# Five slots instead of four for the stacks of split q and k rows, with each load one pair of head pairs further up

## The chip, the cores and the metric

The kernel runs on one core of a Trainium2 chip. The time is device microseconds of one execution, from the first instruction to the last. The engines are called as in the profile: PE is TensorE (matmul) and PEld its weight loads, DVE is VectorE, ACT is ScalarE, POOL is GpSimd, SP is SyncE, which issues nearly all DMAs; SPq is the sequencer of its queue. Each engine runs its instructions in the order in which the program lists them. An instruction that has to wait holds up whatever stands behind it on that engine, and this holds for a DMA that SP issues as well.

## The reference

One transformer block with conditioning. The input is 2048 rows of 512 numbers; attention has 32 heads of 16 and works in four segments of 512 rows, with a memory that is carried from segment to segment.

```python
mod = (_silu(c) @ w_mod).reshape(c.shape[0], 6, 1, -1)          # sa, ca, ga, sb, cb, gb
h = _layernorm(x) * (1 + ca) + sa
x = x + ga * A(h)
h = _layernorm(x) * (1 + cb) + sb
x = x + gb * (gelu(h @ w1 + b1) @ w2 + b2)                      # 512 -> 1792 -> 512

def A(x):                                       # per segment s of 512 rows, per head
    logits = qs @ ks.T * scale + causal_mask
    a_dot  = softmax(logits) @ vs
    a_mem  = (phi(qs) @ M) / (phi(qs) @ z + 1e-6)
    o      = g * a_mem + (1 - g) * a_dot
    M, z   = M + phi(ks).T @ vs, z + sum(phi(ks))
    return concat(o) @ wo
```

## The kernel before

The program has three phases. The first, to about 195 us, does the modulation, the layer norm, the projections to q, k and v and the memory. The rows of q and k are written to DRAM (tiles QD and KD) as three bf16 terms each, so that a bf16 matmul of 96 rows gives a product of the two in higher precision. The third phase, from 495 us, is the feed-forward part.

Between them runs the attention loop. A **stack** is a group of four heads of one segment (two head pairs) whose split q and k rows lie side by side in SBUF; there are 32 stacks, Q = 0 to 31, and 64 head pairs, P = 2Q and 2Q + 1. A stack's rows are loaded by two DMAs (L192) into a slot, which is a pair of tiles `qst` and `kst` of 96 used rows by 4 x 512. Rows 96 to 98 carry the negated row maximum (`m_put`, L676 for q) and ones (for k, filled once per slot by ScalarE, L187). A stack Q uses slot `Q % NK`, with `NK = 4`.

The loop runs over P from -4 to 65. In each step `PRM['order']` lists what every engine gets, in text order: `S` parts compute scores of pair P + 4 (L608, L643) and their row maximum on VectorE (L615), `T` parts compute the transposed scores of pair P (`st_mm`, L694), their exponential on ScalarE (L713, L724) and the causal zeros on GpSimd (L697), and the slots `c0` to `c9` take whatever a table put at position 10P + c. From that table come, among others:

- `load_stacks(Q)` at position 20Q + `PRM['stacks']`, here 20Q - 60, that is at P = 2Q - 6. The first scores of the stack are computed at P = 2Q - 4.
- `pv_part` (L738), the weighted sum of v with a stack's exponentials, and `pv_out`, which evicts it (L131, tile `ts`) and stores it (L749, `TD`).
- for each group U of two stacks: `pv_in` loads sums and denominators back (`dn` L754, `opk` L756) and the memory's part (`amB` L763, and in the last segment its reciprocal denominators `rm` L768); `den` inverts the denominators (L773, L774) and stores them (L776, `RD`); `rb_in` loads them back, spread over 16 rows each (L782, `rbB`); `mem_mix` (L794), `mix` (L787, L789) on GpSimd up to group 12 and on VectorE from 13, `o_hi` (ScalarE, L131, tile `oh`) and `o_lo` (L804) make the output of the group, and `wo_part` (L815) projects it.
- `wo_x` and `wo_out` load x, add the projection and store it (`X2D`, L834).

Memory for the first two slots is taken in the first phase from a ring of four buffers (tag `wm`): qst0, kst0, qst1, kst1. The other slots come at the start of the loop from the pool `wop`. The ring is used again near the end of the loop by `stage_w1` (L839), which stages raw feed-forward weights two blocks at a time; `PRM['w1at']` places `w1r0`, `w1r2`, `w1r4` at P = 58, 59 and 60. They get the ring's buffers in turn: w1r0 that of qst0, w1r2 that of kst0, w1r4 that of qst1. A buffer is handed over when the last instruction that used it has ended; here this is the last L694 of the last stack that used the slot.

Of the kernel before, what the change touches and what calls it, by code (L numbers as in the profile page):

```python
# [41 lines left out]
 'mput': [-14, -15, -13, -13],  # L42
 'mrow0': -19,
 'mput0': -9,
 'stacks': -60,
 'den': [84, 84, 84, 84],
 'dnl': 11,
 'rbl': 7,
# [57 lines left out]
def block_kernel(ctx: ExitStack, tc: tile.TileContext, x, wq, wk, wv, wo, betaq, betam,  # L106
# [22 lines left out]
    def copy(e, dst, src):  # L129
        if e == "a":  # L130
            act.activation(dst, src, AF.Copy)  # L131
        else:
            (v if e == "v" else pool).tensor_copy(dst, src)
# [43 lines left out]
    QD = [[dram.tile([6, 16, 8, 512], BF16, name=f"QD{s}_{g}") for g in range(4)] for s in range(NSEG)]  # L177
    KD = [[dram.tile([6, 16, 8, 512], BF16, name=f"KD{s}_{g}") for g in range(4)] for s in range(NSEG)]
    TERMS = {"q": (slice(0, 3), slice(4, 6), slice(3, 4)), "k": (slice(2, 5), slice(0, 6, 5), slice(1, 2))}
    NK = 4  # L180
    qst, kst = {}, {}

    def new_stack(i, pl=None):
# [5 lines left out]
    def load_stacks(Q):  # L189
        s, g, t = Q // 8, (Q // 2) % 4, Q % 2  # L190
        for st, dd in ((kst[Q % NK], KD), (qst[Q % NK], QD)):
            sp.dma_start(st[:96], dd[s][g].rearrange("c r e n -> (c r) e n")[:, 4 * t:4 * t + 4, :])  # L192
# [393 lines left out]
    with ExitStack() as pb:  # L586
# [69 lines left out]
        def q_of(P, h, i):  # L656
            return qst[P // 2 % NK][:96, 2 * (P % 2) + h, 128 * i:128 * i + 128]

        def k_of(P, h, n):
            return kst[P // 2 % NK][:96, 2 * (P % 2) + h, 0:n]  # L660

# [9 lines left out]
        def m_put(Q):  # L671
# [3 lines left out]
            copy(PRM["mse"], ms, mm[:48, :128])  # L675
            act.dma_start(qst[Q % NK][96:99], ms)  # L676

# [14 lines left out]
        def st_mm(ps, P, h, j):  # L692
            q, k, e = qst[P // 2 % NK], kst[P // 2 % NK], 2 * (P % 2) + h
            pe.matmul(ps, k[:99, e, 128 * j:128 * j + 128], q[:99, e, 128 * j:512], start=True, stop=True)  # L694
# [153 lines left out]
        def at(P, part, f, *a):  # L848
            todo.setdefault((P, part), []).append((f, a))
# [23 lines left out]
        def ap(pos, f, *a):  # L873
            at(pos // 10, pos % 10, f, *a)

        for Q, P in ((2, -4), (3, -2)):
            at(P, 0, new_stack, Q, wop)
        for Q in range(2, 32):
            ap(20 * Q + PRM["stacks"], load_stacks, Q)
# [311 lines left out]
```

## Time and profile before

| what | value |
|---|---|
| time, three runs | 818.09, 818.81, 825.99 us; median 818.81 |
| profiled execution | span 822.1 us; no other time of it is shown |
| PE busy | 795.2 us, 97% |
| DVE, ACT, POOL busy | 498.7, 365.1, 284.7 us |
| DMA moved | 123.02 MB, 150 GB/s on average |
| attention loop, about | 180 to 495 us |
| feed-forward part, about | 495 to 822 us |

A row of a timeline reads: start, length, engine, line, operation, output <- inputs with buffer numbers left out, how many alike in a row, and in brackets the idle time before with the instruction that ended it. A row of the waits reads: who waited, for whom, us in total, times, the longest. On SPq a row is the issue of a DMA and not its transfer.

### The profile page before, as it was taken

How to read it: one execution, taken by the hardware profiler on the slowest of the kernel's cores; microseconds unless marked ns; L12 is line 12 of the kernel's file. 1: busy time of each engine (PE TensorE's matmuls, PEld its weight loads, DVE VectorE, ACT ScalarE, POOL GpSimd, SP SyncE). 2: the span in 40 equal slices, each digit the busy share in tenths (PEclk: the TensorE clock that was granted, in tenths of full speed). 3: DMA queues.
4: the chain of work that ended last, by engine and by line, in shares of the span. 5: the costliest groups of instructions: out<-in, count | busy, mean ns of one | idle time of the engine just before them, and what ended most of it. 6: DMA issues, size and time to landing. Idle time of an engine off the chain costs nothing.

```text
span 822.1 us, 13438 instructions
## 1 busy us (share of the span) xinstructions
PE 795.2 (97%) x4637; PEld 549.7 (67%) x4637; DVE 498.7 (61%) x1341; ACT 365.1 (44%) x670; POOL 284.7 (35%) x508
## 2 busy tenths in 40 slices
PE   9999999999988899989998989999999999999998
PEld 4877777865434345435544547788888888888887
DVE  6685696469877767877787736886443343324223
ACT  4465645565777756766677662223211111211110
POOL 1347365542577545557867651000000000000000
PEclk9999999999999989989999999999999999999999
DMA  9597756595556666667566664734030111003001
GB/s 342 169 312 251 276 183 206 173 360 135 144 144 169 172 182 193 208 187 210 174 172 177 193 185 150 257 103 140 1 103 1 51 51 52 1 0 103 1 1 51
DMA packets 83565, 123.02 MB, mean 150 GB/s; under 512 B 14116, under 2 KB 46244, under 8 KB 82984
## 3 DMA queue, kind: packets, MB, share of 16 engines
q1 hardware_dynamic: 81000, 120.19, 47.2%
q10 hardware_dynamic: 2496, 1.97, 0.8%
q8 instruction: 36, 0.59, 0.3%
q14 instruction: 33, 0.27, 0.1%
HBM read 75.60 MB, written 46.15 MB: 148 GB/s over the span
## 4 chain that ended last, share of the span: by engine, by line
PE 46%; DMA 4%; DVE 2%; ACT 2%; issue 1%; POOL 1%; SPq 1%; ACTq 0%; DVEq 0%
PE acc L1073 17%; PE f1b L989 16%; PE pvb L738 3%; PE att L694 3%; PE att L608 2%; PE mm L815 2%; DMA xb<-in_x 1%; DMA xt<-X2D 1%; ACT pt L713 1%; PE mm L161 1%; DMA rm<-rdd 1%; DMA w1r<-in_w 1%; PE mm L1073 1%; DMA kst<-KD 0%; ACT ts L131 0%
## 5 line engine op out<-in xcount | busy, mean ns | idle before, releaser
L615 DVE CUSTOM_DVE_ANT_0 dump<-att,maskb 128x512 bf16<-128x512 f32 (+2 forms) x384 | 192.2, 552 | 54.9 <-PE att L608 36.5
L713 ACT ACTIVATE pt<-att 128x512 f32<-128x512 f32 x256 | 144.4, 603 | 55.8 <-PE att L694 41.7
L992 ACT ACTIVATE gt<-f1b,b1t 128x512 f32<-128x512 f32 x56 | 38.5, 688 | 245.7 <-PE f1b L989 202.0
L139 DVE CAST gh<-gt 128x512 fp32r<-128x512 f32 x56 | 24.9, 445 | 164.1 <-ACT gt L992 164.1
L697 POOL TENSOR_SCALAR_AFFINE_SELECT pt<-pt 128x256 f32<-128x256 f32 x256 | 98.9, 408 | 54.1 <-ACT pt L713 31.6
L694 PE MATMUL att<-qst,kst 99*128 99x512 bf16 (+3 forms) x512 | 109.2, 306 | 3.3 <-ACT pt L713 2.8
L608 PE MATMUL att<-kst,qst 96*128 96x512 bf16 (+2 forms) x384 | 92.9, 335 | 10.7 <-DMA qst<-QD 8.9
L1073 PE MATMUL acc<-w2h,gh 128*128 128x512 f32 (+1 forms) x224 | 86.6, 387 | 0.0
L1073 PE MATMUL acc<-w2l,gh 128*128 128x512 f32 (+1 forms) x224 | 86.0, 384 | 0.5 <-DVE w2l L140 0.5
L1073 PE MATMUL acc<-w2h,gl 128*128 128x512 f32 (+1 forms) x224 | 85.9, 383 | 0.0
L738 PE MATMUL pvb<-pt,V 128*32 128x512 f32 (+2 forms) x992 | 84.2, 452 | 0.0
L694 PEld LDWEIGHTS <-kst 99*128 99x128 bf16 x512 | 45.2, 99 | 56.4 <-issue 33.1
L989 PE MATMUL f1b<-hodd,w1h 128*128 128x512 f32 x224 | 73.7, 390 | 0.0
L152 POOL TENSOR_SCALAR crs<-cmv 128x4 f32<-128x4 f32 x4 | 1.0, 248 | 172.1 <-DVE cmv L149 172.1
L608 PEld LDWEIGHTS <-qst 96*128 96x128 bf16 x384 | 33.8, 100 | 35.3 <-DMA qst<-QD 11.2
L738 PEld LDWEIGHTS pvb<-pt,V 128*32 128x32 f32 x992 | 25.3, 110 | 45.1 <-issue 41.4
L1073 PEld LDWEIGHTS acc<-w2l,gh 128*128 128x128 f32 x224 | 42.1, 188 | 9.2 <-DVE w2l L140 0.9
L989 PEld LDWEIGHTS f1b<-hodd,w1h 128*128 128x128 f32 x224 | 42.1, 188 | 8.6
L1073 PEld LDWEIGHTS acc<-w2h,gl 128*128 128x128 f32 x224 | 42.1, 188 | 8.3
L1073 PEld LDWEIGHTS acc<-w2h,gh 128*128 128x128 f32 x224 | 42.1, 188 | 8.3
L989 PE MATMUL f1b<-C0hh,w1l 128*128 128x512 f32 x112 | 43.7, 390 | 0.2 <-DVE w1l L140 0.2
L989 PE MATMUL f1b<-C0hl,w1h 128*128 128x512 f32 x112 | 43.7, 390 | 0.0
(214 smaller groups left out, 1540.6 us busy)
## 6 DMA issues: line engine op xcount, KB each, us to landing
kst<-KD SPq DMA_DIRECT2D x32, 384.0 KB
qst<-QD SPq DMA_DIRECT2D x32, 384.0 KB
TD<-ts SPq DMA_DIRECT2D x32, 256.0 KB
QD<-q SPq DMA_DIRECT2D x16, 384.0 KB
KD<-k SPq DMA_DIRECT2D x16, 384.0 KB
wm<-in_wmod SPq DMA_DIRECT2D x20, 256.0 KB
QD<-q SPq DMA_DIRECT2D x16, 256.0 KB
KD<-k SPq DMA_DIRECT2D x16, 256.0 KB
```

What stands on the lines that cost most here:

```text
L139: v.tensor_copy(hi, src)
L161: pe.transpose(ps[:, 128 * b:128 * b + 128], xh[:, b, 128 * d:128 * d + 128], ident)
L608: pe.matmul(ps, q_of(P, h, i), k_of(P, h, 128 * (i + 1)), start=True, stop=True)
L615: v.tensor_tensor_reduce(out=dump[n_dump[0] % 2][:, :n], in0=src, in1=maskb[:, 512 - n:], scale=-1.0, scalar=-4 * NEG, op0=ALU.add, op1=AL ...
L694: pe.matmul(ps, k[:99, e, 128 * j:128 * j + 128], q[:99, e, 128 * j:512], start=True, stop=True)
L697: pool.affine_select(out=t, in_=t, pattern=pattern, compare_op=ALU.is_ge, fill=0.0, base=0, channel_multiplier=-1)
L713: act.activation(pt[:, h, :], ps, AF.Exp, scale=0.25)
L738: pe.matmul(ps[32 * c:32 * c + 32, lo:hi], V[4 * s + j][:, VW * hd:VW * hd + 32], pt[:, c % 2, lo - o:hi - o], start=start, stop=stop)
L815: pe.matmul(ps, a[:, 128 * b:128 * b + 128], w[:, g, :], start=(g == 0 and i == 0), stop=(g == 3 and i == 2))
L989: pe.matmul(ps, a[:, k, :], b[k], start=(i == 0), stop=(i == 11))
L992: act.activation(g, ps, AF.Gelu_apprx_tanh, bias=b1t[:, f:f + 1])
L1073: pe.matmul((mm if lo else acc[b])[:, lo:hi], a[:, c], w[:, lo:hi], start=(f == 0 and i == 0), stop=(last and i == 2))
```

## The change

The load position goes from 20Q - 60 to 20Q - 80 (P = 2Q - 8), there are five slots, and the fifth is made at P = 0 in the pool `wop`.

```diff
- 'stacks': -60,
+ 'stacks': -80,
...
-    NK = 4
+    NK = 5
...
-        for Q, P in ((2, -4), (3, -2)):
+        for Q, P in ((2, -4), (3, -2), (4, 0)):
             at(P, 0, new_stack, Q, wop)
         for Q in range(2, 32):
             ap(20 * Q + PRM["stacks"], load_stacks, Q)
```

What it moves is seen in the order of SP's instructions. In the middle of the loop, at the store of stack 4's sums; KD1_1 and QD1_1 hold stacks 10 and 11, KD1_0 and QD1_0 stacks 8 and 9, and the digit after `kst` or `qst` is the slot. Before:

```order
L192 DMA kst1_1782<-KD1_0_93 96x2048
L192 DMA qst1_1781<-QD1_0_77 96x2048
L749 DMA TD2_2751<-ts4_2752 128x512
L776 DMA RD1_2768<-dn1_2707 128x32
L782 DMA rbB1_2804<-RD1_2768 128x1x512
L192 DMA kst2_2020<-KD1_1_94 96x2048
L192 DMA qst2_2019<-QD1_1_78 96x2048
```

and now, at the same place:

```order
L192 DMA kst0_1777<-KD1_1_94 96x2048
L192 DMA qst0_1776<-QD1_1_78 96x2048
L749 DMA TD2_2756<-ts4_2757 128x512
L776 DMA RD1_2773<-dn1_2712 128x32
L782 DMA rbB1_2809<-RD1_2773 128x1x512
L192 DMA kst1_1782<-KD1_1_94 96x2048
L192 DMA qst1_1781<-QD1_1_78 96x2048
```

The load of stack 10 has moved up to where that of stack 9 stood, past one store of sums (TD) and the pair RD and rbB; stack 11's stands where stack 10's stood. The instructions between keep their order. A load's slot was last used by stack Q - 4 before and by stack Q - 5 now.

At the end of the loop PE's rows keep their order, and only the slots change: pair 61's last transposed scores, a projection, pair 63's first and, after the first v sums of stack 30, its last ones. Before:

```order
L694 MATMUL att4_2010<-qst2_2019,kst2_2020 128x128
L815 MATMUL mm_1983<-woh_1996,oh9_4758 128x512
...
L738 MATMUL pvb_2012<-pt60_0_5561,V12_151 32x512 x2
L738 MATMUL pvb_2012<-pt61_0_5592,V12_151 32x512 x2
...
L694 MATMUL att2_2008<-qst3_2078,kst3_2079 128x128
L738 MATMUL att3_2009<-pt62_0_5647,V12_151 32x512 x2
```

and now:

```order
L694 MATMUL att4_2010<-qst0_1776,kst0_1777 128x128
L815 MATMUL mm_1983<-woh_1996,oh9_4763 128x512
...
L738 MATMUL pvb_2012<-pt60_0_5564,V12_151 32x512 x2
L738 MATMUL pvb_2012<-pt61_0_5595,V12_151 32x512 x2
...
L694 MATMUL att2_2008<-qst1_1781,kst1_1782 128x128
L738 MATMUL att3_2009<-pt62_0_5650,V12_151 32x512 x2
```

Stacks 30 and 31 lay in slots 2 and 3; now they lie in slots 0 and 1, those of the ring. Slot 0's and slot 1's last stacks before were 28 and 29.

The part of SP's order that follows the weights' staging is the same before and after except for the numbers; it reads now:

```order
L839 DMA w1r0_5412<-in_w1 128x4x128 x2
L834 DMA X2D2_123<-xb2_1_5221 128x512
L754 DMA dn13_5449<-TD13_5261 128x1x32
L756 DMA opk13_5451<-TD13_5261 128x1x512
L763 DMA amB13_5453<-AMD3_1_118 128x512
L768 DMA rm13_5455<-rdd3_1968 128x1x512
...
L839 DMA w1r2_5480<-in_w1 128x4x128 x2
L749 DMA TD14_5511<-ts28_5512 128x512
L839 DMA w1r4_5546<-in_w1 128x4x128 x2
L834 DMA X2D2_123<-xb2_2_5341 128x512
L776 DMA RD13_5569<-dn13_5449 128x32
L782 DMA rbB13_5593<-RD13_5569 128x1x512
```

Here w1r0 and w1r4 are the loads whose buffers come from slots 0 and 1; what stands behind them belongs to group 13, to the third segment's output and to stack 28.

## The prediction

> **What bounds the kernel now.** I read the page's busy times first, then the waits of TensorE, then the waits of SyncE's DMA queue, then the timelines of the places that these name. The page, with the span, the busy row and the costliest wait of TensorE's score matmuls:
>
> ```profile
> span 822.1 us, 13438 instructions
> ...
> PE 795.2 (97%) x4637; PEld 549.7 (67%) x4637; DVE 498.7 (61%) x1341; ACT 365.1 (44%) x670; POOL 284.7 (35%) x508
> ...
> L608 PE MATMUL att<-kst,qst 96*128 96x512 bf16 (+2 forms) x384 | 92.9, 335 | 10.7 <-DMA qst<-QD 8.9
> ```
>
> TensorE is busy for 97% of the span, so whatever idle time is taken from it is gained and whatever is added is lost. The program runs it in order, and from 495 us on it is the feed-forward part alone; a delay before that moves the end. The waits of TensorE say what an earlier load can take away at most directly: six waits, 8.9 us.
>
> ```profile
> PE att L608 <- DMA qst<-QD: 8.9, 6, 2.9
> ```
>
> They lie in one stretch. Busy time by stretch (columns: stretch, length, busy time of each engine, granted clock, DMA share, GB/s):
>
> ```profile
> 226.00:304.00 78.00, 68.63 (x545) 31.69 (x543) 54.86 (x206) 52.06 (x105) 46.87 (x99) 0.93 0.61 166
> 304.00:452.00 148.00, 141.75 (x1148) 73.94 (x1146) 114.00 (x420) 101.54 (x202) 99.98 (x195) 0.98 0.65 189
> ```
>
> In 226–304 us TensorE idles 9.4 us and its clock is granted at 0.93; later in the same loop at 0.98. Idle time plus 0.05 × 68.6 = 3.4 us of clock gives 13 us, more than which the head of this loop can't give.
>
> **Part 1: the earlier load, in the head.** The load of stack Q+1 now stands where that of Q stood in SyncE's queue; it waits, as before, for the previous stack of its slot, which with five slots is one stack older. So a load is issued one stack (about two head pairs) sooner, and the six waits for landings (8.9 us) should go. What is late next? SyncE's own queue:
>
> ```profile
> 236.35 0.37 SPq L749 DMA_DIRECT2D TD<-ts  x1
> ...
> 243.55 0.60 SPq L754 DMA_DIRECT2D dn<-TD  x1
> ...
> 247.65 0.34 SPq L776 DMA_DIRECT2D RD<-dn  x1
> 252.82 0.60 SPq L782 DMA_DIRECT2D rbB<-RD  x1
> ...
> 254.48 0.38 SPq L749 DMA_DIRECT2D TD<-ts  x1
> ```
>
> One group of two stacks takes SyncE 254.48 − 236.35 = 18.1 us, and its links are DMA round trips: store TD to load dn 7.2 us, store RD to load rbB 5.2 us. The waits of that queue over the run say the same:
>
> ```profile
> SPq L782 <- DMA RD<-dn: 44.2, 16, 5.0
> ...
> SPq L192 <- PE att L608: 34.1, 15, 14.8
> ```
>
> The slot waits (34.1 us) are what the change shortens; the 44.2 us behind RD stay. And the end of this chain already has a consumer standing there. GpSimd, then ScalarE, in the same group:
>
> ```profile
> 257.31 1.27 POOL L787 TENSOR_TENSOR opk<-opk,rbB 128x512 f32<-128x512 f32 x1 [3.45 <-DMA rbB<-RD]
> ```
>
> ```profile
> 258.62 0.63 ACT L131 ACTIVATE oh<-opk 128x512 fp32r<-128x512 f32 x1 [0.87 <-POOL opk L787]
> ```
>
> GpSimd waited 3.45 us for rbB, and ScalarE 0.87 us for GpSimd, with the exponentials queued behind it. If TensorE came there 2 us earlier per group, ScalarE would wait 2 us longer. I therefore take −4 us, about half of the 8.9 and a third of the 13. The ends are −13 us (all of the loss goes) and 0 (each wait for a load becomes one for rbB).
>
> **Part 2: the fifth slot's fill.** One more fill of 32 rows by ScalarE.
>
> ```profile
> L187 ACT ACTIVATE kst<-one x4: 1887/1904/1905, 161.3 to 188.4; 32x2048 bf16<-32x2048 f32 x4
> ```
>
> It costs 1.9 us on ScalarE at P=0, near 200 us, where the loop's first exponentials are due. ScalarE is busy 44% of the span, so most of it lies beside other work: +0.5 us, between 0 and 1.9. The third extra load in a row in the start (stack 4's) is two DMA issues of about 0.4 us on a queue that then has nothing else due: 0.
>
> **Part 3: the tail.** This is where the sum turns. Slots 0 and 1 share a ring of four buffers with the staging of FFN weights: w1r0 takes the buffer of qst slot 0, w1r2 that of kst 0, w1r4 that of qst 1. Which stack was last in them changes. With four slots, the last in slot 0 is stack 28 and in slot 1 stack 29; with five, they are 30 and 31, the last two of all. So SyncE's w1r0 waited for pair 57's last transposed-score matmul (L694) and now waits for pair 61's; w1r4 waited for pair 59's and now waits for pair 63's, the end of the loop. SyncE is in order. Behind w1r0 stand X2D, dn13, opk13, amB13, rm13, w1r2 and TD14; behind w1r4 another X2D, RD13, rbB13 and all of the last two groups. Before, on SyncE:
>
> ```profile
> 463.25 0.99 SPq L839 DMA_DIRECT2D w1r<-in_w  x2
> 467.51 0.34 SPq L834 DMA_DIRECT2D X2D<-xb  x1
> ...
> 470.49 0.59 SPq L768 DMA_DIRECT2D rm<-rdd  x1
> ...
> 475.31 1.70 SPq L839 DMA_DIRECT2D w1r<-in_w  x2
> ...
> 479.14 0.38 SPq L776 DMA_DIRECT2D RD<-dn  x1
> 483.54 0.60 SPq L782 DMA_DIRECT2D rbB<-RD  x1
> ```
>
> and on TensorE (pair 57's last L694s, pair 61's, the start of stack 30's weighted sum, pair 63's last, stack 31's weighted sum):
>
> ```profile
> 462.25 0.60 PE L694 MATMUL att<-qst,kst 99*128 99x256 bf16 x4
> ...
> 479.62 1.31 PE L694 MATMUL att<-qst,kst 99*128 99x512 bf16 x7
> ...
> 484.21 1.06 PE L738 MATMUL pvb<-pt,V 128*32 128x512 f32 x8
> ...
> 487.40 1.04 PE L694 MATMUL att<-qst,kst 99*128 99x512 bf16 x7
> ...
> 492.03 3.01 PE L738 MATMUL att<-pt,V 128*32 128x512 f32 x28 [2.61 <-POOL pt L697]
> ```
>
> The consumers, on GpSimd, VectorE and ScalarE:
>
> ```profile
> 478.39 1.28 POOL L794 TENSOR_TENSOR amB<-amB,rm 128x512 f32<-128x512 f32 x1 [0.62 <-DMA rm<-rdd]
> ...
> 483.50 1.25 POOL L697 TENSOR_SCALAR_AFFINE_SELECT pt<-pt 128x256 f32<-128x256 f32 x3 [0.57 <-ACT pt L724]
> ```
>
> ```profile
> 487.83 0.69 DVE L787 TENSOR_TENSOR opk<-opk,rbB 128x512 f32<-128x512 f32 x1 [11.43 <-DMA rbB<-RD]
> ```
>
> ```profile
> 489.36 0.63 ACT L131 ACTIVATE oh<-opk 128x512 fp32r<-128x512 f32 x1 [2.49 <-DVE opk L789]
> ```
>
> First hold. w1r0 is released at 479.62 + 1.31 = 480.9 instead of 462.9. It issues for 1.0 us to 482.0; X2D 0.34, dn13 0.6, opk13 0.6, amB13 0.4 bring rm13 to 484.2. From issue to GpSimd's start of L794 it took 478.39 − 470.49 = 7.9 us there, and in the chain of what ended last a later one took 6.1:
>
> ```profile
> 500.16 6.09 DMA rm<-rdd
> ```
>
> So L794 starts at 490.3 to 492.1, lasts 1.28 us, and GpSimd's causal selects of pair 60, three of which stand behind it, take 1.25 us more (as the three at 483.50): stack 30's weighted sum starts at 492.9 to 494.7, middle 493.8, instead of 484.21: +9.6 us. Pair 63's last L694s follow in TensorE's order: 488.44 + 9.6 = 498.0.
>
> Second hold. w1r4 is released at 498.0; it issues in 1.35 us (between the 0.99 and 1.70 above), X2D in 0.34, so that RD13 goes out at about 499.9. Then 483.54 − 479.14 = 4.4 us to rbB13 and 487.83 − 483.54 = 4.3 us to VectorE's mix: 508.6 instead of 487.83, **+20.8 us**. Where these round trips were short, store to load took 2.2 us:
>
> ```profile
> 505.48 0.32 SPq L776 DMA_DIRECT2D RD<-dn  x1
> 507.69 0.59 SPq L782 DMA_DIRECT2D rbB<-RD  x1
> ```
>
> That would make it +18.6. The rest hangs on the mix without slack: ScalarE's oh13 stands ahead of pair 63's exponentials (it waited 2.49 us before too), these gate stack 31's weighted sum, that gates the feed-forward part, which is bound by TensorE to the end.
>
> **Part 4: clock after the two holds.** TensorE idles some 9 to 10 us in each. What a restart costs, from the longest wait in the head:
>
> ```profile
> 278.68 0.50 PE L608 MATMUL att<-kst,qst 96*128 96x384 bf16 x2 [0.73 <-DMA qst<-QD]
> ...
> 281.99 0.39 PE L694 MATMUL att<-qst,kst 99*128 99x512 bf16 x1
> ...
> 289.16 0.82 PE L608 MATMUL att<-kst,qst 96*128 96x384 bf16 x2 [2.95 <-DMA qst<-QD]
> ...
> 293.01 2.36 PE L738 MATMUL pvb<-pt,V 128*32 128x512 f32 x16
> 295.30 0.61 PE L694 MATMUL att<-qst,kst 99*128 99x512 bf16 x1
> ```
>
> The same sequence took 281.99 − 278.68 = 3.3 us after a short wait and 295.30 − 289.16 = 6.1 us after one of 2.95: 2.8 us lost. Against it, the 2.61 us wait at 492.03 shows no such loss. Ends: 0 and 5.7 for two restarts; the holds are long, so they are nearest to the longer wait: +5.7.
>
> The Trainium skill, "TensorE: Matmul & The Clock Gate", section "Part 1: The HAM clock gate", says that TensorE falls to half its clock after about 3.4 us idle and needs about 3.4 us of work to return; an estimate from that is at most 1.7 us lost for each restart, and the sum by it would be 2.3 us lower. This case's trace differs: 2.8 us were lost after only 2.95 us idle.
>
> **Sum.** −4 + 0.5 + 20.8 + 5.7 = +23.0 us on the profiled execution's 822.1 us span. That execution lies inside the three times shown (818.1 to 826.0); on their median, 818.8, it gives **841.8 us**.
>
> **Rivals.**
> A, the forecast: 0.60.
> B, the head gives all it can (−13): speaks for it that SyncE's chain might run ahead once no load holds it; against it, the rbB waits. 818.8 − 13 + 27 = 833: 0.14.
> C, only the first hold counts, because RD13's trip ends beside it: −4 + 0.5 + 9.6 + 2.8 = +8.9, 828: 0.10. Against it stands that w1r4 can't be released before the last L694, which itself comes after the first hold.
> D, everything long: no gain in the head, rm 7.9 us, X2D 1.95 us: +30, 849: 0.06. A part of this is also the case that the change doesn't do what it says, that is that waits for loads only change into waits for rbB: then it is +27, 846.
> E, **faster**: the hold in SyncE's queue doesn't take place, because the weights' load finds its buffer free early. Its point: w1r0 issued before 471 us, where it is past without moving rm13's use at 478.39. Then the head alone counts, −4 to −13, 806 to 815, middle 810. Against it: slot waits do stop SyncE (34.1 us above), and w1r0 went out 0.4 us after pair 57's last L694, as if waiting for it. 0.10.
>
> The Trainium skill, "Perfetto Trace Analysis", section "Identifying Performance Opportunities / Optimization Strategy", reads a gap that repeats on the engine that should be saturated as a possible sign of too few buffers; that speaks for E. The trace agrees in the head (six waits), and is silent on who else uses the buffers.
>
> **How the numbers follow.** A measurement of this kernel can tell about 1% from no change. E below 810.6 is faster, its upper half is the same; C stands on the edge of slower. Faster 0.06, same 0.09, slower 0.85. The range leaves out E and the far end of D, and takes in B, C, the unknown 0 to 5.7 of the clock and 18.6 to 22 of the tail: 827 to 848.
>
> **What would show it.** In the profile after: TensorE's waits for qst near 0 and not 8.9 (part 1), with longer waits of GpSimd or ScalarE on rbB in 226–304; w1r0 leaving SyncE right behind pair 61's last L694, and w1r4 right behind pair 63's; GpSimd's L794 for group 13 waiting over 8 us on rm; two TensorE idles of about 10 us ahead of stack 30's and stack 31's weighted sums; the first f1b matmul some 20 to 25 us later against the loop's start, and the feed-forward part as long as before. It is wrong if w1r0 goes out early, or if SyncE's waits there are covered by other work.

## The result: slower by 2.65%, as forecast

| | before | changed |
|---|---|---|
| median | 820.76 us (818.09 to 825.99, 6 runs) | 844.17 us (841.28 to 845.85, 6 runs) |
| ratio | 1 | 1.0265, 95% interval 1.0233 to 1.0297 |
| span of the profiled execution | 822.1 us | 843.6 us |

The forecast was +23.0 us and 841.8 us; the medians differ by 23.4 us, the two profiled spans by 21.5 us. The range of 827 to 848 us holds the time.

The page of the changed kernel: span, busy times and the granted clock in 40 slices.

```profile
span 843.6 us, 13434 instructions
...
PE 796.7 (94%) x4637; PEld 550.8 (65%) x4637; DVE 498.9 (59%) x1341; ACT 366.7 (43%) x671; POOL 286.0 (34%) x508
...
PEclk9999999999999999999999967999999999999999
```

TensorE is busy 796.7 us, 1.5 us more than before; the span is 21.5 us longer. So nearly all of the loss is idle time, and the two low digits of the clock say where: slices 24 and 25, about 485 to 527 us. The waits of TensorE name it:

```profile
PE att L738 <- POOL pt L697: 12.3, 1, 12.3
PE pvb L738 <- POOL pt L697: 10.1, 1, 10.1
PE att L694 <- ACT pt L713: 6.3, 4, 2.1
PE att L694 <- DMA qst<-ms: 3.6, 3, 1.8
PE att L608 <- ACT pt L713: 2.8, 2, 2.5
```

Before, the first row was the wait for stack loads, 8.9 us in six. That row is gone. In its place stand two single waits of 10.1 and 12.3 us, and further down new ones for the row maxima (`qst<-ms`) and longer ones for exponentials (L713). Before, L694 waited 2.8 us in all for exponentials:

```profile
PE att L694 <- ACT pt L713: 2.8, 3, 1.6
```

What held the two long ones back is seen among the waits of SyncE's queue:

```profile
SPq L839 <- PE att L694: 22.2, 2, 11.9
```

L839 is the staging of the feed-forward weights: it stood 22.2 us, in two waits, for transposed-score matmuls; in the profile before this row is a single wait of 0.3 us. Another 8.3 us, in one wait, it stood for the DMA that writes row maxima into the slot (`qst<-ms`), which is also a user of that buffer. SyncE at the end of the loop:

```profile
460.55 0.32 SPq L749 DMA_DIRECT2D TD<-ts  x1
479.43 0.94 SPq L839 DMA_DIRECT2D w1r<-in_w  x2
480.42 0.49 SPq L834 DMA_DIRECT2D X2D<-xb  x1
...
482.78 0.59 SPq L768 DMA_DIRECT2D rm<-rdd  x1
...
485.45 0.88 SPq L749 DMA_DIRECT2D TD<-ts  x1
498.32 0.92 SPq L839 DMA_DIRECT2D w1r<-in_w  x2
499.36 0.43 SPq L834 DMA_DIRECT2D X2D<-xb  x1
499.89 0.38 SPq L776 DMA_DIRECT2D RD<-dn  x1
503.20 0.60 SPq L782 DMA_DIRECT2D rbB<-RD  x1
```

After the TD store of 460.55 SyncE issues nothing for 18.6 us, and after that of 485.45 nothing for 12 us. Both gaps end with a w1r load. The first is the 8.3 us for the maxima and then 10.3 us for L694, the second 11.9 us for L694. TensorE beside it:

```profile
478.36 1.04 PE L694 MATMUL att<-qst,kst 99*128 99x512 bf16 x7
...
492.27 2.64 PE L738 MATMUL pvb<-pt,V 128*32 128x512 f32 x8 [10.06 <-POOL pt L697]
494.84 1.04 PE L694 MATMUL att<-qst,kst 99*128 99x512 bf16 x4
...
497.25 1.04 PE L694 MATMUL att<-qst,kst 99*128 99x512 bf16 x7
...
511.62 4.40 PE L738 MATMUL att<-pt,V 128*32 128x512 f32 x28 [12.34 <-POOL pt L697]
515.95 0.50 PE L989 MATMUL f1b<-C0hh,w1h 128*128 128x512 f32 x1
```

Pair 61's last L694 ends at 479.40 and w1r0 leaves at 479.43; pair 63's ends at 498.29 and w1r4 leaves at 498.32. The consumers, on GpSimd, VectorE and ScalarE:

```profile
490.59 1.26 POOL L794 TENSOR_TENSOR amB<-amB,rm 128x512 f32<-128x512 f32 x1 [14.08 <-DMA rm<-rdd]
```

```profile
507.42 0.69 DVE L787 TENSOR_TENSOR opk<-opk,rbB 128x512 f32<-128x512 f32 x1 [21.06 <-DMA rbB<-RD]
```

```profile
508.94 0.63 ACT L131 ACTIVATE oh<-opk 128x512 fp32r<-128x512 f32 x1 [12.37 <-DVE opk L789]
```

These are the three rows that were shown of before, with waits of 14.08, 21.06 and 12.37 us instead of 0.62, 11.43 and 2.49. The feed-forward part then takes 843.6 − 515.95 = 327.7 us; before it took 822.1 − 494.97 = 327.1. Nothing of the delay is given back in it.

### The profile page after: what moved, and what is told of

It reads as the page before. It is cut to its first block, busy times and chain, and to the rows that moved or that the text cites. A ratio compares the mean times of both kernels' runs of the same rounds, so it can differ in the third digit from the quotient of the medians.

```text
span 843.6 us, 13434 instructions
## 1 busy us (share of the span) xinstructions
PE 796.7 (94%) x4637; PEld 550.8 (65%) x4637; DVE 498.9 (59%) x1341; ACT 366.7 (43%) x671; POOL 286.0 (34%) x508
## 4 chain that ended last, share of the span: by engine, by line
PE 75%; DMA 9%; DVE 4%; POOL 3%; issue 3%; ACT 3%; SPq 1%; ACTq 0%; DVEq 0%; POOLq 0%
PE acc L1073 17%; PE f1b L989 16%; PE pvb L738 7%; PE att L694 6%; PE att L608 5%; PE q L329 5%; PE k L329 4%; PE mm L815 4%; PE v L480 3%; DMA RD<-dn 2%; DMA rbB<-RD 2%; DMA rm<-rdd 2%; PE nu L452 1%; ACT pt L713 1%; DMA xt<-X2D 1%
## 5 line engine op out<-in xcount | busy, mean ns | idle before, releaser
L713 ACT ACTIVATE pt<-att 128x512 f32<-128x512 f32 x256 | 144.0, 601 | 49.8 <-PE att L694 38.2
L694 PE MATMUL att<-qst,kst 99*128 99x512 bf16 (+3 forms) x512 | 108.8, 305 | 10.0 <-ACT pt L713 6.3
L738 PE MATMUL pvb<-pt,V 128*32 128x512 f32 (+2 forms) x992 | 84.8, 451 | 10.1 <-POOL pt L697 10.1
L694 PEld LDWEIGHTS <-kst 99*128 99x128 bf16 x512 | 44.6, 98 | 60.8 <-issue 33.3
L738 PEld LDWEIGHTS pvb<-pt,V 128*32 128x32 f32 x992 | 25.5, 110 | 55.1 <-issue 40.1
L989 PE MATMUL f1b<-C0hh,w1h 128*128 128x512 f32 x112 | 43.7, 390 | 0.0
```

Of the source, the lines that this page charges most:

```text
L713: act.activation(pt[:, h, :], ps, AF.Exp, scale=0.25)
L738: pe.matmul(ps[32 * c:32 * c + 32, lo:hi], V[4 * s + j][:, VW * hd:VW * hd + 32], pt[:, c % 2, lo - o:hi - o], start=start, stop=stop)
L989: pe.matmul(ps, a[:, k, :], b[k], start=(i == 0), stop=(i == 11))
```

## The experiments

**The tail.** First the changed kernel with the weights staged later, behind what they wait for, and the same in the kernel before as the price of that:

```diff
- 'w1at': [58, 59, 60],
+ 'w1at': [62, 63, 64],
```

> The changed kernel with the staging of w1r0, w1r2 and w1r4 written at P = 62, 63 and 64 instead of 58, 59 and 60, so that each stands behind the last L694 that it waits for; nothing else differs. Theory (the two holds in SyncE's queue are the whole loss): the 10.1 and 12.3 us waits of TensorE ahead of stack 30's and 31's weighted sums go, and with them about 3 us of clock; what is left is the head's gain of 1.3 us at pair 61 (479.4 against 480.9 us), so 818 to 821 us, ratio to before 0.997 to 1.003. Rival 1 (the loss comes from the earlier loads or the fifth slot, and the holds only show where it ends): 835 us or more. Rival 2 (late staging makes the first feed-forward weights late): 823 to 830 us, with a wait of VectorE or TensorE on w1r at the start of the feed-forward part.

> The kernel before with w1r0, w1r2 and w1r4 staged at P = 62, 63 and 64. It prices the late staging by itself. Theory: the weights are needed only from the first f1b matmul on, 495 us, and land by 490 to 492, so no change, ratio 0.997 to 1.003. Rival 2: 2 to 8 us slower, with a wait on w1r at the start of the feed-forward part.

Changed kernel, staged late: 823.4 us, ratio to before 1.003 (0.9999 to 1.0061). Kernel before, staged late: 818.9 us, 0.9983 (0.9953 to 1.0013). Each ratio here and below is to runs of the kernel before that were taken beside it. So 2.65% shrink to 0.3% when three table entries are moved, and rival 1 falls. The waits of TensorE in the changed kernel with late staging, the first four:

```profile
PE att L694 <- DMA qst<-ms: 7.4, 4, 2.5
PE att L694 <- ACT pt L713: 6.4, 3, 3.0
PE att L643 <- ACT pt L713: 2.3, 1, 2.3
PE acc L815 <- ACT oh L131: 2.0, 1, 2.0
```

Both long waits are gone. Rival 2 is half right: from the first f1b matmul to the end this execution took 826.1 − 494.2 = 331.9 us, 4 more than the changed kernel. In the kernel before with late staging the feed-forward part took 818.2 − 487.0 = 331.2 us, 4 more as well, but there the loop's end, from the last transpose of row maxima (L673) to the first f1b, was 15.0 instead of 18.3 us, and the total is the same.

Then one hold of the two, with only w1r4 moved:

```diff
- 'w1at': [58, 59, 60],
+ 'w1at': [58, 59, 64],
```

> The changed kernel with only w1r4 staged late (P = 64); w1r0 and w1r2 stay at P = 58 and 59. This leaves the first hold and takes the second away. Theory: TensorE still waits about 10 us ahead of stack 30's weighted sum, but RD13 goes out at about 487 instead of 499.9 us, and the 12.3 us wait goes, but for at most 3 us: 828 to 832 us, ratio 1.009 to 1.014. Rival (one chain only, and the first hold is covered once the second is gone): within 2 us of before. Rival (the two holds are one, whichever is left costs all): 840 us or more.

835.2 us, ratio 1.0182 (1.0117 to 1.0247): more than the 828 to 832 expected, though the interval reaches down into the expected ratios, and neither rival. TensorE's weighted sums of stack 30 and 31 in it:

```profile
490.28 2.64 PE L738 MATMUL pvb<-pt,V 128*32 128x512 f32 x8 [10.10 <-POOL pt L697]
...
501.15 3.67 PE L738 MATMUL att<-pt,V 128*32 128x512 f32 x28 [3.72 <-POOL pt L697]
```

The first wait is as in the changed kernel, the second falls from 12.3 to 3.7 us, so the two add. The expectation was 3 us at most for the second. What was too small in it is the trip of RD13, whose parts show on SyncE: it went out at 485.78, rbB13 only at 492.78.

```profile
485.78 0.32 SPq L776 DMA_DIRECT2D RD<-dn  x1
492.78 0.60 SPq L782 DMA_DIRECT2D rbB<-RD  x1
```

That is 7.0 us where the tail before took 4.4. It explains the 0.7 us more of the wait; the rest of the miss is within the noise of four runs.

Last, the hold without the fifth slot: the kernel before with the weights two pairs sooner.

```diff
- 'w1at': [58, 59, 60],
+ 'w1at': [56, 57, 58],
```

> The kernel before, four slots and loads where they were, with w1r0, w1r2 and w1r4 staged two pairs sooner, at P = 56, 57 and 58. Now w1r0 stands ahead of pair 57's last L694, which it waits for, and w1r4 ahead of pair 59's: the hold without the fifth slot. Theory: SyncE stands at w1r0 from about 453 to 462.9 us and RD12 and rbB12 behind it go out some 5 to 7 us late; then TensorE waits near stack 28's and 29's weighted sums, 5 to 15 us in all: 825 to 836 us, ratio 1.006 to 1.018. Rival (holds hurt only together with the fifth slot, or at the loop's end): within 2 us of before.

833.6 us, ratio 1.0138 (1.0084 to 1.0191). The size is as expected, the place is not: the largest wait of TensorE is for a stack's load.

```profile
467.41 1.25 PE L608 MATMUL att<-kst,qst 96*128 96x384 bf16 x4 [9.59 <-DMA qst<-QD]
```

The load of stack 31 stood right behind w1r0 in SyncE's queue and was held with it. A hold hurts whatever stands behind it, four slots or five; which consumer waits depends on the queue's order. I had looked for it at rbB12.

**A version without holds, and the head.** Next the five slots and the early loads with the tail cured at its cause: slot 0 is given up after stack 25, so that w1r0 and w1r2 find it free. (The helper makes line numbers 4 higher from here on.)

```diff
+    def slot(Q):
+        return Q % NK if Q < 30 else Q - 29
...
-            ap(20 * Q + PRM["stacks"], load_stacks, Q)
+            ap(20 * Q + (PRM["stacks"] if Q < 30 else -60), load_stacks, Q)
...
- 'w1at': [58, 59, 60],
+ 'w1at': [58, 59, 62],
```

> Five slots and early loads as in the changed kernel, but slot 0 is given up after stack 25: stacks 30 and 31 lie in slots 1 and 2 and are loaded at 20Q - 60, and only w1r4 is staged late (P = 62). So w1r0 and w1r2 wait for pair 51's last L694, long past, and stand at P = 58 and 59 as before. Theory (holds are the tail's whole loss, and late staging cost the feed-forward part 4 us in the run with all staging late): both long waits of TensorE go and the feed-forward part is as short as before; what is left is the head, where the start costs 2 to 4 us and the middle gains 2 to 4: 818 to 823 us, ratio 0.997 to 1.003. Rival (fifth slot or early loads cost something all through the loop): 826 us or more.

820.2 us, ratio 0.9979 (0.9955 to 1.0003). The holds are the tail's whole loss: from the last transpose of row maxima to the first f1b it is 16.3 us here, 18.3 before and 40.5 in the changed kernel, and the feed-forward part takes 818.7 − 491.4 = 327.3 us again. But the six waits for loads, 8.9 us, are gone here too, and the kernel is no faster than before by what can be measured. Where did they go? First, whether slots or place took them away: the same, with the loads at 20Q − 60 as before.

```diff
- 'stacks': -80,
+ 'stacks': -60,
```

> As the run with slot 0 given up, but the loads stand where they were before (20Q - 60): the fifth slot without the earlier place. SyncE's loads then find their slot free for a whole stack. Theory (the loads are late since their place in SyncE's queue is behind rbB and the stores of sums, not since the slot is taken): TensorE's waits for loads, 0 with the early place, come back to 4 to 9 us, and the total is 818 to 822 us. Rival (the slot is what held them): TensorE's waits for loads stay under 2 us.

822.5 us, ratio 1.0043 (1.0018 to 1.0068). TensorE's waits for loads:

```profile
PE att L612 <- DMA qst<-QD: 8.8, 6, 3.0
```

8.8 us in six waits, the longest 3.0: as before with four slots (8.9, 6, 2.9). A free slot alone does nothing for them; the loads came late because of where they stand in SyncE's queue, behind rbB, and with the fifth slot there the earlier place took their waits away. The earlier place with four slots was not run. Against this run the early place (0.9979) is worth 0.64%, some 5 us (2 to 8 us, by the two intervals), and the fifth slot in the old place costs 0.43%, 3.5 us (1.5 to 5.6).

About 2 us of that cost lie in the start. Between the first and the third transpose of the row maxima (L673) TensorE took 203.94 − 192.03 = 11.9 us before, 13.7 us in the changed kernel and 14.3 us in the run just shown. These are the first and third row of each, the kernel before first:

```profile
192.03 0.22 PE L673 MATMUL mm<-identb,nm 128*128 128x128 bf16 x1
...
203.94 0.22 PE L673 MATMUL mm<-identb,nm 128*128 128x128 bf16 x1
```

```profile
192.73 0.22 PE L673 MATMUL mm<-identb,nm 128*128 128x128 bf16 x1
...
198.37 0.61 PE L694 MATMUL att<-qst,kst 99*128 99x512 bf16 x3 [1.46 <-DMA qst<-ms]
...
206.47 0.22 PE L673 MATMUL mm<-identb,nm 128*128 128x128 bf16 x1
```

Three runs look for the cause. The fill alone moved to where ScalarE idled:

```diff
-        for Q, P in ((2, -4), (3, -2), (4, 0)):
-            at(P, 0, new_stack, Q, wop)
+        for Q, P, part in ((2, -4, 0), (3, -2, 0), (4, -1, 5)):
+            at(P, part, new_stack, Q, wop)
```

> As the run with slot 0 given up, but the fill of the fifth slot (1.9 us on ScalarE) stands at P = -1, behind the first row of maxima, where ScalarE idled 3.3 us, instead of P = 0, right ahead of the first exponentials. Theory F (the fill costs the start): the stretch from the first to the third L673, 11.9 us before and 13.7 us in the changed kernel, falls to 12 us, 2 us gained in all. Theory L (stack 4's transfer, in the queues ahead of the 48 rows of maxima, costs it): the stretch stays at 13.5 us or more, and TensorE's first L694 still waits for the maxima's DMA.

820.2 us, 1.0002 (0.9968 to 1.0036). The stretch is 13.3 us and the wait for the maxima stays:

```profile
197.53 0.61 PE L698 MATMUL att<-qst,kst 99*128 99x512 bf16 x3 [1.32 <-DMA qst<-ms]
```

The load alone, written at P = 2:

```diff
-            ap(20 * Q + (PRM["stacks"] if Q < 30 else -60), load_stacks, Q)
+            ap(20 * Q + (PRM["stacks"] if 4 < Q < 30 else -60), load_stacks, Q)
```

> As the run with slot 0 given up, but stack 4 is loaded at P = 2, as it was before, and the fill stays at P = 0. Theory L (its transfer delays the maxima's DMA): the first L694 waits no longer for the maxima and the stretch from the first to the third L673 falls by the wait, but to no less than 12.5 us, since the fill then stands alone ahead of the exponentials. Theory F: the stretch stays at 13.5 us or more. Either way the total moves by 2 us at most.

821.2 us, 0.9989 (0.9962 to 1.0017), and this tells nothing: SyncE had run ahead, waited for nothing, and issued stack 4's load at 187.5 us instead of 187.2. Both together, with the load behind stack 5's, which has to wait:

```diff
-            ap(20 * Q + (PRM["stacks"] if Q < 30 else -60), load_stacks, Q)
+            ap(20 * Q + (-58 if Q == 4 else PRM["stacks"] if Q < 30 else -60), load_stacks, Q)
```

> As the run with slot 0 given up, with both parts of the start changed: the fill of the fifth slot at P = -1, and stack 4's load written behind stack 5's, which waits for stack 0's last L694, so that it really goes out later, at about 203 us instead of 187 us (in the run with only the load's position changed it still went out at 187.5 us, since SyncE had run ahead). Theory L (the third transfer in a row delays the 12 KB of maxima): TensorE's first L694 no longer waits for them (1.3 us in the run with only the fill moved) and the stretch from the first to the third L673 is 11.9 to 12.2 us, as before, against 13.3 us there. Rival: the stretch stays above 13 us, and the delay has another cause. The total moves by 1 to 2 us, 817 to 820 us.

823.4 us, 1.0044 (1.0016 to 1.0072). The load went out at 202.7 us, the wait for the maxima is gone and the stretch is 11.9 us: the third stack transfer in a row, 768 KB, delays the maxima's 12 KB. But the load is then late for its own use. The third and fourth transpose of the maxima stand 11.9 us apart instead of 7.5:

```profile
204.00 0.22 PE L677 MATMUL mm<-identb,nm 128*128 128x128 bf16 x1
...
215.87 0.22 PE L677 MATMUL mm<-identb,nm 128*128 128x128 bf16 x1
```

and among TensorE's waits stands the one load again that came late:

```profile
PE att L612 <- DMA qst<-QD: 2.6, 1, 2.6
```

The delay moved on by one stack and grew: for 3.9 us behind that wait, 211.5 to 215.4, TensorE's clock was granted at 0.56.

In the middle of the head, what came in the place of the loads' waits? In the changed kernel ScalarE waits for GpSimd's mix, and GpSimd for rbB, in the rows of the group that was shown of before:

```profile
259.63 1.26 POOL L787 TENSOR_TENSOR opk<-opk,rbB 128x512 f32<-128x512 f32 x1 [3.47 <-DMA rbB<-RD]
```

```profile
260.93 0.63 ACT L131 ACTIVATE oh<-opk 128x512 fp32r<-128x512 f32 x1 [2.45 <-POOL opk L787]
```

```profile
262.10 0.38 PE L694 MATMUL att<-qst,kst 99*128 99x512 bf16 x1 [2.10 <-ACT pt L713]
```

ScalarE's wait rises from 0.87 to 2.45 us, and 1.2 us behind it TensorE waits 2.10 us for the exponential. So the mix was moved down in the first segment:

```diff
- 'mix': [105, 105, 100, 103],
- 'ohi': [110, 110, 110, 111],
- 'olo': [110, 110, 110, 116],
+ 'mix': [113, 105, 100, 103],
+ 'ohi': [118, 110, 110, 111],
+ 'olo': [118, 110, 110, 116],
```

> As the run with slot 0 given up, but in the first segment mix stands 8 positions further down (113 instead of 105) and o_hi and o_lo too (118 instead of 110). Theory (with loads out of the way rbB is what is late in the head, and ScalarE's oh holds the exponentials): ScalarE's waits of 1.7, 2.5 and 4.0 us for GpSimd's mix in 240-300 us go, with TensorE's waits for exponentials behind them, and the stretch from the sixth to the fourteenth L673, 73 us in the changed kernel and 75.3 at the unhindered 7.5 to 10.1 us for each stack less than that, falls by 4 to 8 us: 812 to 818 us. Rival (rbB is late only since SyncE is slow, and waits move on with it): within 2 us of the run with slot 0 given up.

820.3 us, 0.9982 (0.9953 to 1.0011). TensorE's waits for exponentials do fall, but those for the maxima rise:

```profile
PE att L698 <- DMA qst<-ms: 7.0, 4, 2.2
...
PE att L698 <- ACT pt L717: 2.1, 3, 1.1
```

In the run without the move they were 5.1 and 6.4 us. The rival holds: the time goes from wait to wait. (The expectation's 75.3 us for the unhindered stretch was a slip; eight stacks at 7.5 us are 60.) The start's two edits and the mix's three together:

```diff
+        for Q, P, part in ((2, -4, 0), (3, -2, 0), (4, -1, 5)):
...
+            ap(20 * Q + (-58 if Q == 4 else PRM["stacks"] if Q < 30 else -60), load_stacks, Q)
...
+ 'mix': [113, 105, 100, 103],
+ 'ohi': [118, 110, 110, 111],
+ 'olo': [118, 110, 110, 116],
```

> The same, with the first segment's mix, o_hi and o_lo 8 positions further down. It puts together what the single runs point to. If ScalarE's waits for rbB in the head are what kept the earlier loads from paying (in the profile of the run with only these moved, TensorE's waits for exponentials were 2 us instead of 6), and the start's 2 us come back: 812 to 817 us, ratio 0.990 to 0.996. Rival (the head's time moves from wait to wait, the maxima's DMA next): 818 to 821 us, no difference from before.

819.2 us, 1.000 (0.997 to 1.003). Beside the run with the start's edits alone (1.0044) the moved mix seems worth 0.4%, beside the run with slot 0 given up nothing; what it is worth stays open. No version with five slots beat the kernel before by more than the noise.

What the earlier loads did to the head as a whole is seen in its stretch of 226 to 304 us, in the changed kernel:

```profile
226.00:304.00 78.00, 69.82 (x582) 32.27 (x579) 58.45 (x223) 54.45 (x112) 48.88 (x105) 0.98 0.60 168
```

TensorE idles 8.2 us in it, where it idled 9.4 before: nearly all of the removed waits came back as others. What did change between these two executions is the granted clock, 0.98 instead of 0.93. From the sixth to the fourteenth transpose of the maxima, eight stacks, the changed kernel takes 73.0 us and the kernel before 77.2; of these 4.2 us only 1.2 are idle time, the rest are faster matmuls. Other profiles with the loads in their old place took 73.5 to 74.4 us for the same eight stacks, others with the early place 71.2 to 74.9.

## Why the prediction was right, step by step

**What bounds it: right.** Added TensorE idle time is the loss; the feed-forward part kept its length to 0.6 us.

**Part 1, the head, −4 us: mechanism right, size right partly by luck, one sentence wrong.** The waits for loads went, and waits for rbB through ScalarE's oh came, as named, and beside them waits for the row maxima. The size was taken as half of the 8.9 us of waits. In the two profiled executions the head gained 4.2 us, but 3.0 of them by the clock and 1.2 by idle time; the other profiles show a smaller gain, and the times give 2 to 8 us. Wrong was that the slot waits on SyncE are what the change shortens: they fell only from 34.1 to 30.8 us, and with five slots in the old place the loads were as late as with four.

The Trainium skill, "Perfetto Trace Analysis", section "Identifying Performance Opportunities / Optimization Strategy", says that repeated gaps can mean too few buffers. For these six a buffer alone was not the answer: with one more and the loads in their old place they were 8.8 instead of 8.9 us.

**Part 2, the start, +0.5 us: mis-sized.** It is 1.8 us between the two profiled executions and about 3.5 us by the times. The fill was the smaller part, some 0.5 us of the stretch (13.7 to 13.3 when it was moved) against 1.4 for the load (13.3 to 11.9); the term that was set to 0, the third load in a row, delays the maxima's DMA, for which TensorE then waited 1.1 to 2.3 us in the runs that have it. I had looked at what else SyncE's queue had due, and not at what another engine's queue was moving at that time.

**Part 3, the tail, +20.8 us: right; it was 22.5 at the first f1b with the clock's 3.0 (part 4) in it, so 19.5 by itself.** Counted from the end of pair 61's last L694 (480.93 before, 479.40 after):

| step | before | after | later by | forecast |
|---|---|---|---|---|
| stack 30's weighted sum | +3.28 | +12.87 | 9.6 | 9.6 |
| pair 63's last L694 ends | +7.51 | +18.89 | 11.4 | 9.6, and a restart's clock of 2.8 |
| VectorE's mix of group 13 | +6.90 | +28.02 | 21.1 | 20.8, and 2.8 |
| first f1b | +14.04 | +36.55 | 22.5 | 20.8, and 5.7 |

That the first row fits to 0.1 us is luck: rm13's way from issue to L794 took 7.8 us, the long end of the forecast's 6.1 to 7.9, and the selects behind L794 let TensorE start 0.8 us sooner than forecast. The 19.5 are 1.3 less than 20.8 mainly because RD13 to rbB13 took 3.3 us (499.89 to 503.20) and not 4.4. And of the first hold's 18.6 us the first 8.3 were a wait for the maxima's DMA, which the prediction doesn't have; the release by L694 is as forecast.

**Part 4, the clock, +5.7 us: mis-sized.** Stack 30's eight matmuls took 2.64 instead of 1.06 us and the 24 that follow them 1.50 as before; stack 31's 28 took 4.40 instead of 3.01. That is 1.6 and 1.4 us, 3.0 in all. I took the price from the head, 2.8 us, and put the long holds nearest to it; that step failed. The 2.8 us were clock too: from 289.0 to 295.3 us it was granted at 0.51, and the same matmuls took nearly twice as long as at 278.68 (L738 2.36 instead of 1.28 us). But the slow stretch lasted some 6 us there, after only 2.95 us idle, and behind the first hold 2.8 us, at 0.50, after 10.06. So the longer idle time did not cost more, and why the slow stretches differ in length stays open.

The Trainium skill, "TensorE: Matmul & The Clock Gate", section "Part 1: The HAM clock gate", puts the return at about 3.4 us of work, from which at most 1.7 us a restart was estimated; both restarts here agree with it, while the head's 2.8 us doesn't, and the sum by that page would have been the better one in this term.

**The sum.** Between the two profiled executions it is 0.7 (the loop starts later) + 1.8 (start) − 4.2 (head) + 0.1 (from there to pair 61) + 19.5 + 3.0 + 0.6 (feed-forward part) = +21.5 us, against the forecast's +23.0; the medians differ by 23.4. The start was too cheap by 1 to 3 us, the tail 1.3 and the clock 2.7 us too dear, so the total came out better than its parts, and that is luck.

Rivals B, C and E are out: up to pair 61 head and start together gained 1.5 us and not 13, both holds count, and w1r0 left 0.03 us after the L694 that it was forecast to wait for. Of D two parts came, rm13's long trip and a head in which other waits took the place of those for loads; its X2D of 1.95 us did not (0.49 and 0.43). The time, 844.2 us, lies between A's 841.8 and the 846 to 849 of D.

Open is what the start's DMAs collide on: the delay follows the third stack transfer, but whether in a queue, an engine or at the memory wasn't tried.

## What to carry to other kernels

Where a ring of buffers is shared with a later stage, look at which user holds each buffer last: another modulus changes it, and a load that waits for a buffer holds its whole issuing queue. When a wait on loads is to go, ask first whether the slot or the place in the queue makes them late: here a free slot alone changed nothing, and the earlier place with it did. And before counting a removed wait as a gain, find the next wait of the same chain: 9 us of waits went and the kernel was not faster.

## What the runs showed of the hardware

The restart of TensorE after 10.06 and 12.34 us idle cost 1.6 and 1.4 us. After 3.72 us idle it cost 0.7 us (28 matmuls in 3.67 us, granted clock 0.64), and after 2.61 us none that shows (the same 28 in 3.01 us, granted clock 1.00). After 2.79 us, in the kernel before with the weights two pairs sooner, the same 28 took 3.92 us at a granted clock of 0.59, and after 2.95 us in the head of the kernel before 2.8 us were lost. So in these traces the length of the idle time alone doesn't say what a restart costs.

A DMA of 12 KB on ScalarE's queue landed so much later that TensorE waited 1.1 to 2.3 us for it when a third pair of loads of 384 KB each had been issued on SyncE's queue 5 to 6 us ahead of it; with two pairs it did not wait.
